# Storing the first blocks' column parts one step later, behind the reads of a pair's moves

## The chip, the core and the metric

The kernel runs on one core of a Trainium2 chip. The metric is the device time of one execution in microseconds, lower is better. The core has five engines that run side by side: TensorE (PE, matmuls), VectorE (DVE), ScalarE (ACT), GpSimd (POOL) and SyncE (SP), which here issues nearly all DMA transfers. Each engine takes its own instructions in program order, and waits on the others through semaphores.

## The reference

A block of a transformer: layer norm, then linear attention and a squared-ReLU MLP side by side, both added to the input. There are 2,048 tokens of 512 values, 32 heads of 16, and a hidden width of 1,376.

```python
xn = layernorm(x)
q, k, v = split_heads(xn @ wqkv)             # H = 32, Dh = 16
pq, pk = phi(q), phi(k)                      # phi(t) = where(t > 0, t + 1, exp(t)) + 1e-6
kv  = einsum("bhsd,bhse->bhde", pk, v)       # sums over all tokens
z   = einsum("bhsd->bhd", pk)
o   = einsum("bhqd,bhde->bhqe", pq, kv) / (einsum("bhqd,bhd->bhq", pq, z)[..., None] + 1e-6)
out = x + merge_heads(o) @ wo + (relu(xn @ w1 + b1) ** 2) @ w2 + b2
```

## The kernel before

The tokens are cut into 16 tiles of 128 rows, and four tiles make a block. Every matmul operand is held as a high and a low part (suffixes `h` and `l`), and a product is three matmul passes over these parts.

The order of work is written out by hand: nothing is rescheduled, and each engine runs its instructions in the order in which the program names them. The first third of the time is a loop over steps i = 2 to 15, one tile a step. It computes the keys of tile i and adds to the sum over all tokens that linear attention needs. A step's instructions for TensorE are:

- `project(i)`, 12 matmuls (line 370): the keys of tile i, from the tile's column parts `xs0` or `xs1`, into `pk`;
- for the first tiles, four transposes on TensorE (`pt`, line 309);
- `kx(i - 1)`, 12 matmuls (line 390): the tokens of the tile before times its keys.

The column parts of tile i are its normalised values turned by 128 x 128 and split into high (ScalarE, line 325) and low (VectorE, line 328). Block 0 (tiles 0 to 3) uses `xs1`, block 1 (tiles 4 to 7) `xs0`, block 2 again `xs1`, and so on. So `xs1` is overwritten from tile 8 on (in step 6) and `xs0` from tile 12 on (in step 10). `transposed(i)` does the turn. Tiles 0 to 4 are turned by TensorE. From tile 5 on the turn takes another way, through DRAM:

- the normalised tile, `xp`, is written to a DRAM buffer `via` (`regroup`, line 282). From tile 6 on, tiles go in pairs: (6, 7), (8, 9), ... In the text, via(7) or via(9) is the write of the pair that ends with that tile, issued in the step that normalises it;
- `regroup` also lists four reads `xg<-via`, each for 32 partitions. The text calls them the pair's moves. They are issued by `move()` at the head of the next step (line 290), and the first waits on SP until the write has landed;
- VectorE turns 32 x 32 blocks of the regrouped tile in SBUF (line 294), and then the high and low parts are made as before.

A tile i + 2 of this kind is transposed at the end of step i, so tile 6 at the end of step 4, and tile 8 at the end of step 6.

SP also issues, in this loop: the stores of the turned tiles 0 to 7 to `xTd` (line 337, each at the end of its `transposed`), the loads of `b1s` at the head of step 5 (ahead of `move()`), and the two stores `xsd` for each of blocks 0 and 1, 1 MB each, high and low parts. These keep the column parts of those blocks for the second half of the kernel, which reads them back (`xs0h<-xsd1h` and so on, issued from 223 us on). `fetch()` issues up to three loads of `wo` and `wqkv` pieces ahead; in steps 3 to 10 it has three outstanding and issues none.

After the loop, and until the end, the kernel computes queries, the hidden layer and the sums into the output, for two blocks at a time, twice. This part is not touched by the change.

Of the kernel before, what the change touches and what calls it, by code (L numbers as in the profile page):

```python
# [18 lines left out]
def kernel(  # L19
# [30 lines left out]
    nc = tc.nc  # L50
# [6 lines left out]
    TB = 4  # L57
# [20 lines left out]
    def bank(name, tag="ps"):  # L78
        return psum.tile([P, 512], F32, name=name, tag=tag)
# [14 lines left out]
    def four(name, tag, dt=F32, pool=None):  # L94
        return (pool or work).tile([P, TB, 512], dt, name=name, tag=tag)

    def pair(name):
        return keep.tile([P, 2, 512], F32R, name=name, tag=next_tag("pair"))

    def f32(ap):  # L100
        return ap.bitcast(F32)
# [15 lines left out]
    def split(h, l, src, eh, el):  # L117
        copy(eh, h, src)
        ENG[el].tensor_tensor(out=l, in0=src, in1=f32(h), op=OP.subtract)  # L119
# [27 lines left out]
    xsd = [[dram.tile([P, NJ, BT], F32, name=f"xsd{b}{u}") for u in "hl"] for b in range(NB // 2)]  # L147
# [25 lines left out]
    def units(f):  # L173


        if f < NF - 1:
            return [(0, f * P, P)]
        return [(0, f * P + Q, 2 * Q), (2 * Q, f * P, Q), (3 * Q, f * P, Q)]

    def raw_1(f):  # L180
        t = w512(f"r1_{f}", "raw", 6)
        tj = t.rearrange("p (j n) -> p j n", j=NJ)
        for a, o, n in units(f):
            nc.sync.dma_start(tj[:, :, a:a + n], w1[:, o:o + n].rearrange("(j p) n -> p j n", j=NJ))
        return t
# [47 lines left out]
    def statistics(*tiles):  # L233
        g = group(*tiles)
        measure(g)
        return g

    def roots(tiles, st, mv, y):

        n = len(tiles)  # L240
        nc.scalar.activation(y[:, 1, :n], mv[:, :n, 1], AF.Ln, bias=eps)
        nc.scalar.activation(y[:, 0, :n], y[:, 1, :n], AF.Exp, scale=-0.5)
# [44 lines left out]
    def move(n=8):  # L287
        for _ in range(n):
            if moves:
                nc.sync.dma_start(*moves.pop(0))  # L290
# [9 lines left out]
    def cols(i):  # L300

        return xsb[(i // TB + 1) % 2]
# [10 lines left out]
    def transposed(i, n=1):  # L313

        b, at = i // TB, slot(i)
        if i < NDVE:
            t = turned_pe(i, n)
        else:
            t = [xT[b][:, :, at] if i >= NPE else w512(f"t{i}", "p", 6).rearrange("p (j t) -> p j t", j=NJ)]
            turn(t[0], xg[i])  # L320
        m = NJ // n
        h, l = ([x[:, k * m:(k + 1) * m, at] for k in range(n)] for x in cols(i))

        def high(k=0):
            nc.scalar.activation(h[k], t[k], AF.Copy)

        def low(k=0):
            nc.vector.tensor_tensor(out=l[k], in0=t[k], in1=f32(h[k]), op=OP.subtract)

        def keep_t():  # L330
            o = t[0]
            if i < NDVE:
                o = w512(f"t{i}", "p", 6).rearrange("p (j t) -> p j t", j=NJ)
                for k in range(n):
                    copy("act", o[:, k * m:(k + 1) * m], t[k])
            if i < NPE:
                nc.sync.dma_start(xTd[b][:, :, at], o)

        return high, low, keep_t

    def run(*what):
        for f in what:
            f()
# [23 lines left out]
    def project(i, ps, w, steps, first=True, last=True):  # L367

        for n, (j, u, v) in enumerate(steps):
            nc.tensor.matmul(ps, lhsT=cols(i)[u][:, j, slot(i)], rhs=w[v][:, j, :], start=first and n == 0,  # L370
                             stop=last and n == len(steps) - 1)
# [8 lines left out]
    def phi_k(i, ps, mid=lambda: None, late=lambda: None):  # L380
        kp[i] = w512(f"k{i}", "p", 6)
        phi(ps, kp[i], mid, late)
# [159 lines left out]
    for i0 in range(0, NT, TB):  # L542
# [6 lines left out]
        if i0 < NPE:  # L549
            i = i0 + TB - n - 1  # L550
# [4 lines left out]
        for k in range(0, n, 2):  # L555
            i = i0 + TB - n + k
            u, v = (t.rearrange("p a (g c) -> p (a g c)", g=NJ) for t in (a[:, TB - n + k:][:, :2], o[:, k:k + 2]))
            groups[i + 1] = [t.rearrange("p (g n) -> p g n", g=NJ) for t in (u, v)]
            u, v = (t.rearrange("p (g i c) -> p g i c", g=NJ, i=2) for t in (u, v))
# [87 lines left out]
    def tokens_sum(n, tag):  # L647
        return keep.tile([P, 2, 2, 512], F32R, name=f"T{n}", tag=tag)
# [13 lines left out]
    def halves(t):  # L662

        return t[:, :2], t[:, 2:]
# [16 lines left out]
    def fetch():  # L681
        while todo and len(held) < 3:
            held.append(todo.pop(0)())
# [16 lines left out]
    def load_1(kind, n):  # L700
        load = raw_1 if kind == "w" else raw_q
        return [load(2 * n + k).rearrange("p (c n) -> p c n", c=2) for k in range(2)]
# [30 lines left out]
    def sums_of(f1, f2, o3, o4):  # L733


        o, sums = {}, []

        def sum_1(j):
            o[1] = difference(1, j, f2[:, j], f1[:, j])
            difference_high(1, j, o[1])  # L740

        def sum_2(j):
            o[2] = difference(2, j, f2[:, 2 + j], o[1])
            difference_high(2, j, o[2])

        for j in range(2):
            sums += [lambda j=j: sum_1(j), lambda j=j: sum_2(j),
                     lambda j=j: difference(4, j, f1[:, 2 + j], o[2], o4[:, j]),
                     lambda j=j: difference(3, j, f2[:, 2 + j], f2[:, j], o3[:, j]),
                     lambda j=j: difference_low(1, j, o[1]), lambda j=j: difference_low(2, j, o[2])]  # L750
        return sums

    def operands_first(n, w):

        o = {}

        def first():
            aop.update({k: keep.tile([P, 2, 2, 512], F32R, name=f"aop{n}_{k}", tag=f"xT{NB // 2 + k}") for k in range(2)})
            chunk_split(0, 0, w[0])

        def sums():
            o[0], o[1] = chunk_sums(0, w)

        return [first, sums, lambda: chunk_split(0, 1, o[0]), lambda: last_split(0, w[1][:, 1]),
                lambda: chunk_split(1, 0, o[1])]
# [7 lines left out]
    def more(i=None):  # L773

        if i is None or i > 12:
            do(extra, counts[0].pop(0))
# [6 lines left out]
    for i in range(2, NT):  # L783
        if i == 5:
            nc.sync.dma_start(b1s[:, :NF - 1], b1[:(NF - 1) * P].rearrange("(f p) -> p f", p=P))
            for a, o, n in units(NF - 1):
                nc.sync.dma_start(b1s[a:a + n, NF - 1:], b1[o:o + n, None])
        move()
        fetch()
        ps = pks[i] if i < 3 else bank(f"pk{i}")  # L790
        if i > 2:
            project(i, ps, wk, HL)
        high = low = keep_t = lambda: None
        if i < NDVE:
            high, low, keep_t = transposed(i + 1)

        soon_turned = transposed(i + 2) if 11 <= i and i + 2 < NT else ()

        def mid():
            high()  # L800
            more(i)

        def late():
            if soon:
                roots(*soon)
            low()
            more(i)

        if i == 12:
            rawz = raw_1(NF - 1)  # L810
            T.update({n: tokens_sum(n, f"B{n - 1}") for n in (1, 2)})
        if i == 12:
            w = load_1("q", 0)
        if i == 13:
            todo_1 = operands_first(0, w)
            extra.append(todo_1.pop(1))
        if i == 14:
            z = pair("w1z0")
            extra.append(lambda: split(z[:, 0], z[:, 1], rawz, "act", "dve"))
            o34 = halves(four("Tf", "r0"))  # L820
            extra.extend(sums_of(xT[NB - 1], xT[NB - 2], *o34))
            lows = [extra.pop() for k in range(2)]
            extra += [todo_1[0], lows[1], todo_1[1], lows[0], *todo_1[2:]]
        phi_k(i, ps, mid, late)
        more(i)
        run(*soon_turned)
        later = normalise(*soon) if soon else []
        parts(i)
        keep_t()
        if i == 2:  # L830
            tokens(2)
        if i + 1 < NT:
            tokens(i + 1)
        run(*later)
        if NDVE < i + 2 < 13:
            run(*transposed(i + 2))
        pieces([3, 1, 1, 2, 1][i - 11] if i > 10 else 0)
        if i == 2:
            ahead[3] = statistics(6, 7)
        if i + 2 in (4, 6, 8, 10):  # L840
            ahead[i + 2] = group(i + 6, i + 7)
        if i < 10:
            measure(ahead[(i + 2) // 2 * 2], i % 2)
        soon = ahead.get(i + 1, ())
        if i in (3, 6):

            b = i // 6
            for u in range(2):
                nc.sync.dma_start(xsd[b][u], f32(cols(b * TB)[u]))
        kx(i - 1)  # L850
        more(i)

# [52 lines left out]
    for n in range(2):  # L905
# [339 lines left out]
        for e, f in enumerate(waiting[:-2]):  # L1245
# [14 lines left out]
            if n == 0 and 1 <= e < 5:  # L1260
                k, u = divmod(e - 1, 2)
# [68 lines left out]
```

## Time and profile before

| | |
|---|---|
| time, median of 3 runs | 419.6 us (419.21 to 420.58) |
| time of the profiled execution | 419.62 us |
| its span, first to last instruction | 417.9 us |
| TensorE busy | 409.5 us, 98% |
| VectorE, ScalarE, GpSimd busy | 315.5, 269.9, 49.0 us |
| mean granted TensorE clock | 0.996 of full |
| DMA, mean over the span | 132 GB/s |

How to read what follows: the page's engine rows give busy time, share of the span and number of instructions. A row of the waits names the waiting instruction, what it waited for, the total in us, how often, and the longest. A row of a timeline gives start in us, duration in us, engine, line, operation, output and input, number of merged instructions, and in brackets the idle time before it with what ended it. Here `SPq` is SP's issue of a DMA; its duration is that of the issue, not of the transfer. A row of the chain gives start, duration and what. A row of the windows gives the stretch, its length, the busy time of PE, PE's weight loads, DVE, ACT and POOL with their instruction counts, and then the granted clock, the busy share of the DMA engines and GB/s. For one tile the durations are min/median/max, in ns for instructions and in us for the time from a DMA's issue to its landing.

### The profile page before, as it was taken

Reading aid. Unit: us, or ns where it says so; the run is one execution under the profiler, and the core shown is the slowest. Engines: PE = TensorE matmul, PEld = TensorE weight load, DVE = VectorE, ACT = ScalarE, POOL = GpSimd, SP = SyncE. Lnnn points to the kernel's source line nnn. Section 1 sums busy time; section 2 is a strip of 40 time slices with the busy share of each in tenths; the row PEclk is TensorE's granted clock in tenths of the full one; section 3 lists DMA queues with packets and bytes.
Section 4 is the critical chain, followed back from the end, with each engine's and each line's share of the span. In section 5 each row is a group of like instructions: output and inputs, shape, how many; then the busy total and the mean of one; then the engine's idle time right before and its main releaser. Section 6 shows DMA issues by size and latency. Waiting matters only on the chain.

```text
span 417.9 us, 5430 instructions
## 1 busy us (share of the span) xinstructions
PE 409.5 (98%) x1831; PEld 338.2 (81%) x1831; DVE 315.5 (75%) x585; ACT 269.9 (65%) x486; POOL 49.0 (12%) x70
## 2 busy tenths in 40 slices
PE   8998899999999999999999999999999999999996
PEld 7786788878888888888878888888888888878885
DVE  6893766699699898997539997467998685449843
ACT  5864776764778778889565732467678857737420
POOL 3241221221040000011000040100000200000210
PEclk9999899999999999999999999999999999999999
DMA  7869482460231222346076991511231781025602
GB/s 244 289 230 345 128 301 100 140 189 1 66 112 51 51 76 78 100 152 101 14 314 226 343 249 49 165 52 25 55 94 30 217 186 50 2 77 175 102 0 100
DMA packets 45645, 55.15 MB, mean 132 GB/s; under 512 B 7985, under 2 KB 29745, under 8 KB 44338
## 3 DMA queue, kind: packets, MB, share of 16 engines
q1 hardware_dynamic: 43314, 50.61, 37.5%
q0 software_dynamic: 2304, 4.20, 6.3%
q8 instruction: 14, 0.23, 0.2%
q14 instruction: 13, 0.11, 0.1%
HBM read 41.43 MB, written 13.37 MB: 131 GB/s over the span
## 4 chain that ended last, share of the span: by engine, by line
PE 93%; DMA 3%; DVE 1%; SPq 1%; ACT 1%; issue 0%; DVEq 0%
PE acc L130 36%; PE b L489 32%; PE pk L370 10%; PE kx L390 9%; PE acc L500 2%; DMA xg<-via 1%; PE pz L130 1%; PE pkv L881 1%; SPq L290 1%; PE pm L130 1%; DMA via<-xp 1%; PE pz0b L130 1%; PE b L130 1%; DMA x<-in_A_x_dram 1%; PE pt L309 0%
## 5 line engine op out<-in xcount | busy, mean ns | idle before, releaser
L130 PE MATMUL acc<-w2r,s 128*128 128x512 f32 x477 | 112.8, 390 | 0.0
L130 PEld LDWEIGHTS acc<-w2r,s 128*128 128x128 f32 x477 | 89.5, 188 | 19.2 <-issue 0.7
L489 PE MATMUL b<-T,aop 128*128 128x512 f32 x336 | 83.4, 390 | 0.0
L489 PEld LDWEIGHTS b<-T,aop 128*128 128x128 f32 x336 | 63.1, 188 | 13.1
L390 PE MATMUL kx<-pk,tok 128*128 128x512 f32 x192 | 46.6, 392 | 0.0
L390 PEld LDWEIGHTS kx<-pk,tok 128*128 128x128 f32 x192 | 36.0, 189 | 8.2 <-issue 0.4
L489 PE MATMUL b<-xs0h,aop 128*128 128x512 f32 x112 | 36.9, 391 | 0.0
L130 PE MATMUL acc<-mh,aTsr 128*128 128x512 f32 x112 | 35.7, 390 | 0.0
L1011 POOL DMA_DIRECT2D res<-in_B_b_dram x16 | 14.1, 1065 | 181.7 <-DVE dt L431 64.3
L119 POOL TENSOR_TENSOR tok<-xp,tok 128x512 fp32r<-128x512 f32 x16 | 21.4, 1342 | 61.9 <-ACT tok L111 61.9
L1019 DVE TENSOR_TENSOR res<-acc,res 128x512 f32<-128x512 f32 x16 | 11.0, 692 | 23.1 <-PE acc L130 18.4
L122 DVE TENSOR_TENSOR w2r<-r,w2r 128x512 fp32r<-128x512 f32 (+2 forms) x35 | 25.6, 734 | 0.1
L130 PEld LDWEIGHTS acc<-mh,aTsr 128*128 128x128 f32 x112 | 21.0, 188 | 4.4
L489 PEld LDWEIGHTS b<-xs0h,aop 128*128 128x128 f32 x112 | 21.0, 188 | 4.3
L111 ACT ACTIVATE aop<-S 128x512 fp32r<-128x512 f32 x28 | 17.5, 624 | 10.6 <-DVE S L710 10.6
L119 DVE TENSOR_TENSOR aop<-S,aop 128x512 fp32r<-128x512 f32 x28 | 19.5, 698 | 4.8 <-ACT aop L111 4.4
L119 DVE TENSOR_TENSOR s<-c,s 128x512 fp32r<-128x512 f32 x20 | 13.6, 690 | 11.5 <-ACT s L111 11.4
L130 PE MATMUL acc<-ml,aTsr 128*128 128x512 f32 x56 | 21.8, 390 | 0.0
L489 PE MATMUL b<-xs0l,aop 128*128 128x512 f32 x56 | 21.8, 390 | 0.0
L111 ACT ACTIVATE w2r<-r 128x512 fp32r<-128x512 f32 x32 | 19.6, 618 | 2.2 <-DMA out_dram<-res 2.0
L111 ACT ACTIVATE T<-Tf 128x512 fp32r<-128x512 f32 x16 | 9.5, 626 | 16.9 <-DVE Tf L653 16.7
L489 PE MATMUL b<-xs1h,aop 128*128 128x512 f32 x56 | 19.5, 390 | 0.0
(197 smaller groups left out, 771.8 us busy)
## 6 DMA issues: line engine op xcount, KB each, us to landing
r<-in_B_w_dram SPq DMA_DIRECT2D x49, 256.0 KB, 3.0
res<-in_A_x_dram SPq DMA_DIRECT2D x8, 512.0 KB, 4.7
res<-in_B_b_dram POOLq DMA_DIRECT2D x16, 256.0 KB, 5.4
out_dram<-res SPq DMA_DIRECT2D x15, 256.0 KB, 2.0
x<-in_A_x_dram SPq DMA_DIRECT2D x5, 512.0 KB, 5.2
via<-xp SPq DMA_DIRECT2D x5, 512.0 KB, 2.7
xg<-via SPq DMA_DIRECT2D x20, 128.0 KB, 3.5
xTd<-t SPq DMA_DIRECT2D x8, 256.0 KB, 3.0
```

Source lines behind the costliest of these rows:

```text
L111: nc.scalar.activation(o, i, AF.Copy, bias=bias)
L119: ENG[el].tensor_tensor(out=l, in0=src, in1=f32(h), op=OP.subtract)
L122: nc.vector.tensor_tensor(out=l, in0=src, in1=f32(h), op=OP.subtract)
L130: nc.tensor.matmul(ps, lhsT=a[u], rhs=b[v], start=first and n == 0, stop=last and n == 2)
L290: nc.sync.dma_start(*moves.pop(0))
L370: nc.tensor.matmul(ps, lhsT=cols(i)[u][:, j, slot(i)], rhs=w[v][:, j, :], start=first and n == 0, stop=last and n == len(steps) - 1)
L390: nc.tensor.matmul(kxp[c], lhsT=tok[i][:, u, c * P:(c + 1) * P], rhs=pk[i][:, v], start=i == 0 and (u, v) == first, stop=i == NT - 1 and ( ...
L489: nc.tensor.matmul(ps, lhsT=a[u][:, j * P:(j + 1) * P], rhs=b[v][:, j, :], start=first and j == 0 and n == 0, stop=last and j == 1 and n == 2,
L500: nc.tensor.matmul(ps, lhsT=s[u][:, k * P:(k + 1) * P], rhs=w2s[NF - 1][u][:, a:z], start=first and u == 0, stop=stop and u == 1)
L881: nc.tensor.matmul(ps[:, at], lhsT=wvs[:, c, at], rhs=kxs[c // 2][:, c % 2, at], start=c == 0 and j == 0, stop=c == NJ - 1 and j == NJ - 1 ...
L1011: nc.gpsimd.dma_start(r[:, i], b2[None, :].partition_broadcast(P), accum_op=OP.add)
L1019: nc.vector.tensor_tensor(out=r[:, a:z], in0=ps, in1=r[:, a:z], op=OP.add)
```

## The change

The two stores `xsd` of a block are taken from the end of step 3 (block 0) and step 6 (block 1), where they stand ahead of `kx(i - 1)`, and put at the head of steps 4 and 7, between `move()` and `fetch()`. The code between the old and the new place issues no DMA other than the moves. For SP this is an exchange: four moves and two stores change places, twice. The data, the sizes, the queue and all work of the other engines are as before.

```diff
@@ -786,6 +786,11 @@
         move()
+        if i in (4, 7):
+
+            b = i // 7
+            for u in range(2):
+                nc.sync.dma_start(xsd[b][u], f32(cols(b * TB)[u]))
         fetch()
...
@@ -842,11 +847,6 @@
         soon = ahead.get(i + 1, ())
-        if i in (3, 6):
-
-            b = i // 6
-            for u in range(2):
-                nc.sync.dma_start(xsd[b][u], f32(cols(b * TB)[u]))
         kx(i - 1)
```

## The prediction

> **What bounds the kernel now.** I read the page first, then the waits of TensorE, the chain of waits, and the timelines of the engines around the place that the chain points to.
>
> ```profile
> span 417.9 us, 5430 instructions
> PE 409.5 (98%) x1831; PEld 338.2 (81%) x1831; DVE 315.5 (75%) x585; ACT 269.9 (65%) x486; POOL 49.0 (12%) x70
> ...
> PE 93%; DMA 3%; DVE 1%; SPq 1%; ACT 1%; issue 0%; DVEq 0%
> ```
>
> TensorE is busy for 409.5 of 417.9 us and carries 93% of the chain, so a change of DMA order can only pay where TensorE stands still or runs slowly. Its waits over the whole run name one such place; all others are 0.8 us or less. The timeline of TensorE gives the place, the windows its clock.
>
> ```profile
> PE pk L370 <- ACT xs0h L325: 3.3, 1, 3.3
> PE warm L520 <- PEq L1316: 0.8, 1, 0.8
> ...
> 36.86 2.88 PE L390 MATMUL kx<-pk,tok 128*128 128x512 f32 x12
> 43.01 0.50 PE L370 MATMUL pk<-wkh,xs0h 128*128 128x512 f32 x1 [3.27 <-ACT xs0h L325]
> ...
> 44.00:47.40 3.40, 3.40 (x9) 2.61 (x9) 2.40 (x5) 1.44 (x4) 1.02 (x1) 0.51 0.53 91
> 47.40:50.00 2.60, 2.60 (x13) 2.15 (x12) 2.06 (x5) 2.07 (x5) 0.35 (x2) 0.98 0.75 227
> ```
>
> The 12 matmuls of kx(4) end at 36.86 + 2.88 = 39.74. The next instruction, the first of project(6), starts at 43.01, 3.27 us later, because the high part of tile 6 is missing. One microsecond after the gap the granted clock falls to 0.51 for 3.4 us, and then it is back at 0.98. The chain shows what tile 6 waits for (start, duration, what).
>
> ```profile
> 29.63 2.74 DMA via<-xp
> ...
> 32.39 0.74 SPq L290
> ...
> 35.77 5.69 DMA xg<-via
> ...
> 41.58 0.72 DVE t L294
> ...
> 42.33 0.64 ACT xs0h L325
> ...
> 43.01 4.61 PE pk L370 x12
> 47.62 2.73 PE kx L390 x12
> 50.34 2.72 PE pk L370 x12
> ```
>
> The pair (6, 7) is written to DRAM at 29.63, has landed at 32.37, and its four moves xg<-via are issued from 32.39. The last is issued at 35.77 and lands at 41.46. Then VectorE turns tile 6, ScalarE takes its high part, and TensorE goes on. After the gap project takes 4.61 us where the next one, at 50.34, takes 2.72. The whole price of the stall is 3.27 + (4.61 - 2.72) = 3.27 + 1.89 = 5.16 us. What stands ahead of the moves is seen in SP's timeline.
>
> ```profile
> 30.65 0.74 SPq L849 DMA_DIRECT2D xsd0h<-xs1h  x1
> 31.44 0.45 SPq L849 DMA_DIRECT2D xsd0l<-xs1l  x1
> 32.39 4.56 SPq L290 DMA_DIRECT2D xg<-via  x4
> 36.99 0.52 SPq L337 DMA_DIRECT2D xTd<-t  x1
> 37.62 0.65 SPq L282 DMA_DIRECT2D via<-xp  x1
> 42.32 0.53 SPq L337 DMA_DIRECT2D xTd<-t  x1
> 42.90 0.62 SPq L785 DMA_DIRECT2D b1s<-in_B_b_dram  x1
> 43.57 1.88 SPq L787 DMA_DIRECT2D b1s<-in_B_b_dram  x3
> 45.55 1.79 SPq L290 DMA_DIRECT2D xg<-via  x4
> ...
> 53.01 0.42 SPq L849 DMA_DIRECT2D xsd1h<-xs0h  x1
> 53.52 0.74 SPq L849 DMA_DIRECT2D xsd1l<-xs0l  x1
> 55.30 3.98 SPq L290 DMA_DIRECT2D xg<-via  x4
> 63.15 0.34 SPq L282 DMA_DIRECT2D via<-xp  x1
> ```
>
> Two stores of 1 MB each go out at 30.65 and 31.44, inside the time in which SP would only wait for the landing at 32.37; the moves stand behind them. The same four moves cost as follows without stores ahead (first pair of lines, the moves at 45.55) and with them (second pair, those at 32.39): issue durations, then issue to landing.
>
> ```profile
> L290 SPq DMA_DIRECT2D xg<-via x4: 367/430/432, 45.5 to 46.9; - x4
> ...
> DMA to landing us min/median/max: 2.4/2.6/2.7
> ...
> L290 SPq DMA_DIRECT2D xg<-via x4: 737/1210/1270, 32.4 to 35.8; - x4
> ...
> DMA to landing us min/median/max: 5.7/6.7/7.4
> ```
>
> From first issue to last landing that is 46.9 - 45.5 + 2.7 = 4.1 us in quiet, and 41.46 - 32.39 = 9.07 us behind the stores.
>
> **The change, part by part.** No instruction is added or removed. Four DMA issues move past eight, in two places.
>
> First place, step 4. The moves still can't start before 32.39, since via(7) lands at 32.37. With nothing ahead of them they take the quiet 4.1 us: landed at 36.5. Had they to share the DMA engines with the stores that now follow from about 34.2 (32.39 + 1.79), the far end is today's 41.46; I take the quiet value, since the stores come after them in the same queue.
>
> ```profile
> 34.76 0.69 DVE L378 SCALAR_TENSOR_TENSOR pk<-k,pk 128x512 fp32r<-128x512 f32 x1
> 41.58 0.71 DVE L294 STREAM_TRANSPOSE t<-xg 128x512 f32<-128x512 f32 x1 [6.12 <-DMA xg<-via]
> ...
> 45.87 0.69 DVE L378 SCALAR_TENSOR_TENSOR pk<-k,pk 128x512 fp32r<-128x512 f32 x1 [0.75 <-ACT pk L111]
> ...
> 35.16 1.51 ACT L259 ACTIVATE xp<-x,y 128x512 f32<-128x512 f32 x2
> ```
>
> VectorE is free from 35.45 and ScalarE from 36.67, so nothing else holds tile 6. Landing to TensorE took 43.01 - 41.46 = 1.55 us; 36.5 + 1.55 = 38.05 is 1.7 us before project(6) is due at 39.74. The gap goes, and with it the slow stretch behind it. What could be late next is kx(5), due at 39.74 + 2.72 = 42.46. Its last operand, the low part of pk(5), ended 45.87 + 0.69 - 42.33 = 4.23 us after the high part of tile 6 began; that would be 37.3 + 4.2 = 41.5, which is 0.9 us early. So the first place gives 5.16 us.
>
> The stores now stand behind the moves and ahead of the store xTd of tile 5 and of via(9), the pair (8, 9). Nobody waits for tile 5's store until the second half. But via(9) is the next pair's way to TensorE:
>
> ```profile
> DMA to landing us min/median/max: 5.7/5.7/5.7
> ...
> 32.40:37.60 5.20, 5.20 (x25) 4.31 (x24) 2.54 (x7) 3.81 (x8) 1.34 (x2) 1.00 1.08 398
> ```
>
> The first line is via(9) of before: it landed at 37.62 + 5.7 = 43.3, already behind stores and moves (ScalarE's xp lets it start no sooner than 36.67). The block of stores and moves ahead of it now begins with the moves at 32.39 and not with the stores at 30.65, so it starts 1.74 us later and I let via(9) land as much later, at 45.1. The near end is 43.3, if the engines catch up. The b1s loads, which held SP until 45.45, are now issued inside this wait, since the store of tile 6 ahead of them no longer waits for the late turn. The moves of pair (8, 9) then go out at 45.1 instead of 45.55 and land at 45.1 + 4.1 = 49.2. TensorE is 5.16 us earlier, however: project(8) is due at 39.74 + 4 x 2.72 = 50.62, and needs the landing by 50.62 - 1.55 = 49.07. That leaves 0.1 us of stall. The tile store xTd(6) and b1s may now still drain ahead of these moves: 256 KB at the 398 GB/s of the last column is 0.66 us, of which I take half. I put the new stall at 0.35 us. Its ends: nothing, if via(9) lands at 43.3; and 3 us more, if these moves land in 5.7 us (the best of the congested row) and not 2.7, which is 3.1 us.
>
> Second place, step 7: the stores at 53.01 and 53.52 go behind the moves at 55.30. They filled a wait of SP there too, and the moves behind them held VectorE, not TensorE, which has no wait in this stretch. Moves that land sooner give nothing. The stores go out some 4 us later, at 57.1 (55.30 + 1.79), ahead of the via issued at 63.15. Were that block to drain no faster than the one in step 4, in 9.07 us, the via would land 3 us later; I cost it at zero, because the pair behind stores in this same stretch cost TensorE nothing.
>
> The stores themselves read xs1, which step 6 overwrites with tile 8's parts. They were issued 1 us before the moves' wait ended; behind 1.79 us of moves they go out at 34.2 to 35.4 and precede via(9) in the queue, so tile 8, which needs via(9), comes after them. No wait is added there.
>
> Sum, against the profiled execution's 419.62 us (span 417.9, and 1.7 us around it; the median of the runs is 419.6): 419.62 - 5.16 + 0.35 = 414.8 us.
>
> **The rivals.** (a) *The gap moves one pair on, and is larger.* The moves of pair (8, 9) meet the stores that now come 3.5 us later: if they take the 9.07 us measured behind stores, they land at 45.1 + 9.1 = 54.2, project(8) stalls 54.2 - 49.1 = 5.1 us and the clock falls again for 1.89: 419.62 - 5.16 + 5.1 + 1.89 = 421.5 us. It decides from a landing at 49.07 + 3.27 = 52.3 on. For it: the margin computed above is nil. Against it: SP issues those moves only after via(9) has landed, and via(9) follows the stores in the queue, so the stores are gone by then. (b) *The same, in part*: a stall of 1 to 3 us at project(8), too short for the clock: 415.5 to 417.5. (c) *The stores take the engines anyhow*, and the moves land no sooner than 41.46 although issued ahead: 419.6. Against it: issue alone shrinks from 4.56 to 1.79 us, and what is issued first has the engines alone for 1.8 us. (d) *The slow clock stays*: the stretch of 0.51 is not due to the gap; then only 3.27 comes back: 414.8 + 1.89 = 416.7. The row speaks against it, with full clock on both sides and the fall right after the only gap of that size.
>
> The Trainium skill, page "TensorE: Matmul & The Clock Gate", section "What's actually happening", has the clock halve after at least one idle window of about 3.4 us. By that rule a gap of 3.27 us would be too short, and (d) would hold. The trace disagrees: the clock was 0.51 after just that gap.
>
> **How the numbers follow.** Forecast, with a new stall of 0 to 1 us: 0.72. (a) 0.09, (b) 0.10, (c) 0.06, (d) 0.03. A measurement here can tell about 0.3%, 1.3 us, from no change: faster means below 418.3. Forecast, (b) and (d) are faster, 0.85; (c) is the same, 0.06; (a) is slower, 0.09. The range starts at 414.0, which is no new stall (414.5) less the 0.4 us by which runs of before lie under their median, and reaches to 417.0, which takes in (d) and most of (b) and leaves out (a), (c) and the end of (b), under 0.2.
>
> **What would show it.** In the changed kernel's SP timeline the four moves at about 32.4 should take about 1.8 us with the stores behind them, and the turn of tile 6 should start at about 36.6. TensorE should have no wait at project(6) and no clock below 0.9 from 36 to 50, and kx(4) to kx(5) should be 5.44 us apart. The moves of pair (8, 9) should land at about 49, and a wait at project(8), if any, should be under 1 us. The forecast is wrong if tile 6 still lands after 38.2, if a wait of over 1 us stands at project(8), or if the half clock is seen without a gap ahead of it.

## The result, and the profile after

The changed kernel takes 414.12 us (median of 4 runs, 414.02 to 414.55) against 419.47 us before (4 runs, 419.21 to 420.58). The ratio is 0.987, with a 95% interval of 0.985 to 0.9889: 5.4 us faster. The forecast was 414.8 us in a range of 414.0 to 417.0. The profiled execution took 414.14 us, with a span of 412.4 us, which is 5.5 us less.

The page of the kernel after: span, engines, the granted clock in 40 slices, and the chain by engine.

```profile
span 412.4 us, 5429 instructions
...
PE 407.2 (99%) x1831; PEld 336.9 (82%) x1831; DVE 315.4 (76%) x585; ACT 269.8 (65%) x486; POOL 49.1 (12%) x70
...
PEclk9999999999999999999999999999999999999999
...
PE 97%; DVE 1%; DMA 1%; ACT 0%; issue 0%
```

DMA has fallen from 3% to 1% of the chain, and no slice shows a lower clock. Before, the fifth slice did:

```profile
PEclk9999899999999999999999999999999999999999
```

TensorE's waits of the kernel after, longest first:

```profile
PE warm L520 <- PEq L1316: 0.8, 1, 0.8
PE pt L309 <- DVE y L250: 0.7, 1, 0.7
PE pk L370 <- ACT xs1h L325: 0.3, 1, 0.3
```

The wait of 3.3 us on `xs0h` is gone, and nothing has taken its place. SP's timeline of the kernel after shows the exchange:

```profile
32.64 1.73 SPq L290 DMA_DIRECT2D xg<-via  x4
34.41 0.43 SPq L793 DMA_DIRECT2D xsd0h<-xs1h  x1
34.89 0.43 SPq L793 DMA_DIRECT2D xsd0l<-xs1l  x1
...
36.72 1.08 SPq L282 DMA_DIRECT2D via<-xp  x1
37.90 1.23 SPq L337 DMA_DIRECT2D xTd<-t  x1
39.18 1.44 SPq L785 DMA_DIRECT2D b1s<-in_B_b_dram  x1
40.68 3.33 SPq L787 DMA_DIRECT2D b1s<-in_B_b_dram  x3
44.11 1.79 SPq L290 DMA_DIRECT2D xg<-via  x4
```

From issue to landing, these four moves:

```profile
DMA to landing us min/median/max: 2.3/2.6/2.7
```

The moves take 1.73 us to issue instead of 4.56, and 2.7 us at most to land instead of 7.4. The transfers behind the stores pay for it: the issue of via(9) takes 1.08 us instead of 0.65, and that of the b1s loads 4.8 us instead of 2.5. VectorE's turns of tiles 6 and 8 show what that does:

```profile
36.76 0.71 DVE L294 STREAM_TRANSPOSE t<-xg 128x512 f32<-128x512 f32 x1 [1.28 <-DMA xg<-via]
...
48.49 0.71 DVE L294 STREAM_TRANSPOSE xT<-xg 128x512 f32<-128x512 f32 x1 [1.89 <-DMA xg<-via]
```

and so does the chain, from kx(4) on:

```profile
36.98 2.72 PE kx L390 x12
39.70 2.72 PE pk L370 x12
42.42 2.72 PE kx L390 x12
...
50.58 2.72 PE pk L370 x12
```

Tile 6 is turned at 36.76 instead of 41.58. Tile 8's moves now make VectorE wait 1.89 us, where it did not wait before. But project(8) still starts on time, at 50.58, and from kx(4) on TensorE runs through at 2.72 us for each group of 12, so kx(4) and kx(5) are 5.44 us apart, as forecast.

Where the 5.46 us between the two chains' last pieces (414.44 before, 408.98 after) come from can be read off: 5.20 us are gained by the start of project(8) (55.78 against 50.58). The rest is at kx(12), the 12 matmuls behind project(13); the chain has it so before:

```profile
85.72 2.98 PE kx L390 x12
```

and so after:

```profile
80.50 2.74 PE kx L390 x12
```

With the 0.02 us of issue ahead of the first, that is 0.26 us. (The expectations below call these matmuls kx(13), which is a miscount by one.)

### The profile page after: what moved, and what is told of

Same layout as the page of the kernel before. It is cut to its first block, busy times and chain, and to the rows that moved or that the text cites. A ratio compares the mean times of both kernels' runs of the same rounds, so it can differ in the third digit from the quotient of the medians.

```text
span 412.4 us, 5429 instructions
## 1 busy us (share of the span) xinstructions
PE 407.2 (99%) x1831; PEld 336.9 (82%) x1831; DVE 315.4 (76%) x585; ACT 269.8 (65%) x486; POOL 49.1 (12%) x70
## 4 chain that ended last, share of the span: by engine, by line
PE 97%; DVE 1%; DMA 1%; ACT 0%; issue 0%
PE acc L130 37%; PE b L489 32%; PE pk L370 11%; PE kx L390 11%; PE acc L500 2%; PE pz L130 1%; PE pkv L881 1%; PE pm L130 1%; PE pz0b L130 1%; PE b L130 1%; DMA x<-in_A_x_dram 1%; PE pt L309 1%; PE acc L507 0%; DVE st L230 0%; PE end L130 0%; DVE xp L269 0%
```

## The experiments

In each diff below, `...` stands for lines left out, and the comments are the document's.

**Which of the two places.** Each place was changed alone. The first alone, against the changed kernel:

```diff
-        if i in (4, 7):
+        if i == 4:
...
+        if i == 6:                 # block 1's two stores stay at the end of step 6
```

> Only block 0's stores go behind the moves of step 4; block 1's stay at the end of step 6. Theory: the whole gain comes from the first place, so 414.1 us, no wait of TensorE at project(6), and VectorE waits some 2 us for the moves of the pair (10, 11) as before the change. Rival (the second place pays for the 0.3 us that the gain exceeded 5.16 by, because a store ahead of moves in step 6 disturbs a later pair): 414.4 us, with kx(13) at 2.98 us instead of 2.72.

Measured: 414.38 us (414.21 to 414.84), ratio 0.9882 (0.9866 to 0.9899). The chain has project(6) and kx(12) so:

```profile
39.79 2.72 PE pk L370 x12
...
80.59 2.72 PE kx L390 x12
```

There is no wait at project(6), and kx(12) takes 2.72 us, where the rival gave 2.98. So the theory holds by the chain; the time alone could not tell 414.1 from the rival's 414.4. VectorE's wait for tile 10 was 0.94 us, where some 2 us were expected.

The second alone, against the changed kernel:

```diff
-        if i in (4, 7):
+        if i == 7:
...
+        if i == 3:                 # block 0's two stores stay at the end of step 3
```

> Block 0's stores stay at the end of step 3; only block 1's go behind the moves of step 7. Theory: no gain, 419.5 us, with the 3.3 us wait at project(6) and half clock after it. Rival (the second place is worth 0.3 us): 419.2 us, and kx(13) takes 2.72 us.

Measured: 420.67 us median (417.84 to 421.2, 10 runs), ratio 1.0022 (1.0005 to 1.0039), with the 3.3 us wait at project(6). The same two groups in the chain of the profiled run, which took 419.24 us:

```profile
42.85 4.60 PE pk L370 x12
...
85.59 2.72 PE kx L390 x12
```

So the stall stays and there is no gain, as expected. But kx(12) takes 2.72 us here too, which was the rival's sign. The 0.26 us at kx(12) are gone with either place changed alone, so these runs put them to neither, and 0.3 us can't be told in this spread of times. The spread was not expected, and it goes with the mean granted clock of the run: 417.84 us at 1.000, 419.24 at 0.994, 419.84 at 0.996, and 420.6 to 421.2 at 0.990 or 0.991. Why seven of the ten runs had 0.990 or 0.991 is open. This is taken up below.

**How much of the stores stands ahead.** Block 0's stores were left ahead of the moves by one, by one and a half, and by three (a third one to a spare buffer that nobody reads).

```diff
+        if i == 3:                 # one ahead (the other behind the moves of step 4)
+            nc.sync.dma_start(xsd[0][0], f32(cols(0)[0]))
...
+            nc.sync.dma_start(xsd[0][1][:, :2], f32(cols(0)[1])[:, :2])   # one and a half
...
+            nc.sync.dma_start(spare, f32(cols(0)[1]))                     # three: both and this one
```

> One of block 0's two stores (1 MB) stays ahead of the moves, the other goes behind them; block 1's stores as after the change. Theory (the moves wait for the bytes ahead of them): four moves take 4.1 us with nothing ahead and 9.1 us with 2 MB, so 6.6 us with 1 MB: landed at 39.0, 0.8 us later than the 38.2 that TensorE can bear, a gap of 0.8 us without a fall of the clock: 414.9 us. Rival (any store ahead costs the whole, since the moves then share the engines with one): gap 3.3 us, 419.5 us. Second rival, the slow clock has another cause: half clock near 44 us without a gap of 3 us ahead of it, 416.8 us.

> One and a half of block 0's stores (1.5 MB) stay ahead of the moves, the last half goes behind; block 1's stores as after. Theory: 7.8 us to landing, a gap of 2.1 us at project(6). If the clock falls only after a gap of some 3 us, 416.2 us with full clock throughout; if a gap of 2 us is enough to halve it for 3.4 us, 418.1 us. Rival (any store ahead costs the whole): 419.5 us.

> All of block 0's stores stay ahead of the moves, and a third store of 1 MB, to a DRAM buffer that nobody reads, is added behind them and ahead of the moves; block 1's stores as after. Theory: 11.6 us to landing, a gap of 5.8 us at project(6). If the half clock lasts one stretch of 3.4 us whatever the gap, its price stays at 1.9 us and the time is 419.5 + 2.5 = 422.0 us; if the clock stays low for longer after a longer gap, two stretches cost 3.8 us and the time is 423.9 us. Rival (the stores' bytes are not what delays the moves, but the first store's presence): 419.5 us.

Measured: 415.04 us (414.64 to 415.15), ratio 0.9895 (0.9879 to 0.9911), with one store; 416.71 us (415.89 to 418.62, 9 runs), ratio 0.9943 (0.9923 to 0.9962), with one and a half; 422.23 us (421.82 to 422.47), ratio 1.0052 (1.0035 to 1.0069), with three. The first matmul of project(6) in TensorE's timeline, and the whole of project(6) in the chain, with one store ahead:

```profile
40.21 0.50 PE L370 MATMUL pk<-wkh,xs0h 128*128 128x512 f32 x1 [0.52 <-ACT xs0h L325]
```

```profile
40.21 3.02 PE pk L370 x12
```

with one and a half:

```profile
41.98 0.50 PE L370 MATMUL pk<-wkh,xs0h 128*128 128x512 f32 x1 [1.78 <-ACT xs0h L325]
```

```profile
41.98 3.02 PE pk L370 x12
```

and with three (its line numbers are one higher, for the line that makes the spare buffer):

```profile
45.33 0.80 PE L371 MATMUL pk<-wkh,xs0h 128*128 128x512 f32 x1 [5.68 <-ACT xs0h L326]
```

```profile
45.33 5.36 PE pk L371 x12
```

The gap grows with the bytes ahead: 0, 0.52, 1.78, 3.27 and 5.68 us for 0, 1, 1.5, 2 and 3 MB, where 0, 0.8, 2.1, 3.3 and 5.8 were expected. That is about 2.6 us for each MB beyond the first. Each gap is that of the one profiled run; with one and a half stores the runs at full clock lie between 415.89 and 417.6 us, so there it differs from run to run. "Any store ahead costs the whole" is refuted. A gap that leaves the clock alone still costs 0.3 us more than its length, because project(6) takes 3.02 us instead of 2.72.

With three stores the clock was low for longer, as the windows show (the granted clock is the third number from the end):

```profile
40.00:43.40 3.40, 0.00 (x0) 0.00 (x0) 0.00 (x0) 0.00 (x0) 0.00 (x0) 1.00 1.00 248
43.40:50.60 7.20, 5.27 (x13) 4.16 (x14) 4.52 (x8) 3.53 (x6) 1.36 (x2) 0.53 0.64 180
50.60:54.00 3.40, 3.40 (x17) 2.78 (x16) 2.83 (x9) 2.87 (x7) 0.02 (x1) 1.00 0.36 104
```

A mean of 0.53 over 7.2 us is some 6.8 us at half clock (7.2 x 0.47 / 0.5), two stretches of 3.4. Up to 1.9 us of it fall into the gap, which ends at 45.33. So project(6) lost only 5.36 - 2.72 = 2.64 us, between the 1.9 and 3.8 us that the expectation held against each other, and the time came out near the 422.0 us forecast for one stretch although there were two.

**The prediction's rival (a) made real.** Block 0's stores go behind via(9), and so ahead of the next pair's moves.

```diff
-        if i in (4, 7):
+        if i == 7:                 # block 1 as after; block 0 at the end of step 4:
...
+        if i == 4:
+            for u in range(2):
+                nc.sync.dma_start(xsd[0][u], f32(cols(0)[u]))
         kx(i - 1)
```

> Block 0's stores go to the end of step 4, behind via(9) and ahead of the moves of the next pair (8, 9); block 1's stores as after. This is the prediction's rival (a) made real: stores ahead of the moves of a pair, one pair on. Theory: via(9) now has nothing ahead of it and lands in under 3 us, by 39.6; the moves of (8, 9) go out only after the loads of b1s, near 43, and the stores ahead of them are done by about 45, so they land near 48, under the 49.1 that project(8) needs: 414.1 us, at most 0.5 us more. Rival (a): these moves take 9.1 us from there, land at 52 or later, project(8) stalls for 3 us and the clock halves: 419 us.

Measured: 417.44 us (415.75 to 417.8), ratio 0.9933 (0.9909 to 0.9957). My expectation was wrong: the gap did move one pair on, though with a smaller size than rival (a) gives. SP's timeline in this kernel:

```profile
38.25 0.64 SPq L850 DMA_DIRECT2D xsd0h<-xs1h  x1
...
39.44 1.12 SPq L785 DMA_DIRECT2D b1s<-in_B_b_dram  x1
40.59 4.14 SPq L787 DMA_DIRECT2D b1s<-in_B_b_dram  x3
44.78 1.84 SPq L290 DMA_DIRECT2D xg<-via  x4
```

the turn of tile 8 on VectorE:

```profile
50.71 0.71 DVE L294 STREAM_TRANSPOSE xT<-xg 128x512 f32<-128x512 f32 x1 [3.95 <-DMA xg<-via]
```

and the first matmul of project(8):

```profile
52.14 0.50 PE L370 MATMUL pk<-wkh,xs1h 128*128 128x512 f32 x1 [1.46 <-ACT xs1h L325]
```

The moves of (8, 9) go out at 44.78 because the b1s loads hold SP until then: issued behind the stores, these four loads take 5.3 us of SP's time instead of 2.5. But that is only 0.7 us later than in the changed kernel (44.11), and tile 8 is turned 2.2 us later (50.71 against 48.49). The rest is in the time from issue to landing of these moves, here and then in the changed kernel:

```profile
DMA to landing us min/median/max: 2.5/2.9/4.3
```

```profile
DMA to landing us min/median/max: 2.4/2.7/2.8
```

TensorE waits 1.46 us at project(8), and 1.0 us more at kx(7). To tell the b1s loads from the stores' bytes, the loads were moved to step 9, here and in the changed kernel.

```diff
-        if i == 5:                 # the four b1s loads, ahead of move()
+        move()
+        if i == 9:                 # the same four loads, behind move()
```

> As the kernel with block 0's stores at the end of step 4, with the four b1s loads moved from the head of step 5 to step 9, behind its moves. That kernel took 417.4 us because the moves of (8, 9) went out only at 44.8 and landed at 50.6. Theory (SP was held by the b1s loads, 5.3 us of issue behind the stores): the moves now go out from 39.6 on, when via(9) lands, and are in by about 46 to 48, no wait at project(8): 414.2 us. Rival (the stores' own bytes ahead of these moves are the cause, as in step 4 before the change): landed 9.1 us after via(9), near 49 or later, project(8) still waits: 415 to 417.5 us.

> The changed kernel, with the four b1s loads moved from the head of step 5 to step 9, behind its moves. Theory: TensorE has no wait left that hangs on them, so the time stays at 414.1 us within 0.3; the moves of (8, 9) go out when via(9) lands and VectorE's wait of 1.9 us for them becomes shorter. Rival (the b1s loads still cost TensorE something, through a late tile 8): 413.8 us or less.

Measured: 414.42 us (413.99 to 414.85), ratio 0.9877 (0.9858 to 0.9896), with the stores at the end of step 4, and 414.23 us (414.21 to 415.05), ratio 0.9879 (0.9856 to 0.9901), for the changed kernel. In the first, the moves of (8, 9) in SP's timeline:

```profile
39.51 4.62 SPq L290 DMA_DIRECT2D xg<-via  x4
```

and tile 8's turn in VectorE's:

```profile
48.69 0.71 DVE L294 STREAM_TRANSPOSE xT<-xg 128x512 f32<-128x512 f32 x1 [2.18 <-DMA xg<-via]
```

Tile 8 comes 2 us sooner, and the wait at project(8) is gone: the b1s loads ahead of the moves made the difference. Whether they did it by the time for which they held SP or also by their own transfers isn't separated. The moves themselves are as slow behind the stores as the rival had it: from 39.51 to about 48.6 is 9.1 us, the same as before the change. Issued that early, they are still in time. In the changed kernel the loads are worth nothing, as expected; neither version beats it. Without the loads its moves of (8, 9) go out when via(9) has landed:

```profile
44.31 1.74 SPq L290 DMA_DIRECT2D xg<-via  x4
```

That is no earlier than with them (44.11), in a run whose earlier moves went out 0.5 us later (33.12 against 32.64). So in the changed kernel the loads held these moves for only some 0.3 us beyond the landing of via(9).

**The clock by itself.** The kernel before, with 12 more matmuls for TensorE in the gap, whose result is overwritten.

```diff
+        if i == 6:
+            for n in range(12):
+                nc.tensor.matmul(ps, lhsT=wk[0][:, n % NJ, :P], rhs=wk[0][:, n % NJ, :], start=True, stop=True)
         if i > 2:
             project(i, ps, wk, HL)
```

> The kernel before, with 12 more matmuls whose result is overwritten (2.7 us of work for TensorE) ahead of project(6), where it otherwise stands idle for 3.3 us. The stores and moves stay as before. Theory: tile 6 comes no sooner, so the gap's own 3.3 us stays, but TensorE is idle for only 0.6 us of it and its clock doesn't fall: project(6) takes 2.7 to 3.0 us instead of 4.6, clock 1.00 in every run, 417.6 to 418.0 us. Rival (the slow stretch has another cause than the idle time): half clock near 44 us all the same, 419.5 us or more.

Measured: 419.22 us (418.74 to 419.66, 10 runs), ratio 0.9984 (0.9969 to 1.0). The clock is as expected, with a mean of 0.998 to 1.000 in every run; the size of the gain is not. In the profiled run 0.54 us of the gap are left idle. The windows:

```profile
44.00:47.40 3.40, 3.40 (x16) 2.63 (x15) 2.39 (x5) 1.43 (x4) 1.03 (x1) 1.00 0.55 84
```

VectorE's turn of tile 10:

```profile
63.86 0.71 DVE L294 STREAM_TRANSPOSE xT<-xg 128x512 f32<-128x512 f32 x1 [2.34 <-DMA xg<-via]
```

and project(10) in the chain:

```profile
65.29 3.06 PE pk L370 x12
```

The clock stays at 1.00 between 44 and 47.4. But via(11) goes out at 52.61 as before the change, since VectorE and ScalarE are no earlier. So tile 10, whose moves stand behind block 1's stores, is now late for TensorE: project(10) starts with a wait of 0.3 us and takes 3.06 us, and part of the gain is lost. Adding the second place of the change tests that.

```diff
+        if i == 6:                 # the filled gap, as above
...
+        if i == 7:                 # block 1's stores behind the moves of step 7
```

> The kernel with the filled gap (12 matmuls whose result is overwritten, ahead of project(6)), and block 1's stores behind the moves of step 7 as in the changed kernel; block 0's stores stay ahead of the moves of step 4. With the filled gap alone TensorE won 1.9 us at project(6), and gave some 0.6 us back at project(10), whose tile waits for moves behind block 1's stores. Theory (the second place matters as soon as TensorE is early enough): project(10) starts without a wait and takes 2.72 us, 418.6 us against 419.2. Rival (the second place never matters; the 0.6 us have another cause): 419.2 us, with project(10) as late as in the kernel with the filled gap.

Measured: 417.96 us (417.61 to 420.31, 10 runs), ratio 0.9964 (0.9944 to 0.9984). Eight runs had a mean clock of 0.999 or 1.000 and took 417.61 to 418.29 us; the other two had 0.996 and took 420.15 and 420.31.

The same row of the chain in this kernel:

```profile
65.22 2.72 PE pk L370 x12
```

project(10) no longer waits. The two profiled runs, both near full clock, are 0.8 us apart (417.91 and 418.74), where 0.6 was expected; the medians are 1.3 us apart, but the two kernels ran on different chips, and the intervals of their ratios overlap. kx(12) is back at 2.72 us here, where it took 3.00 with the filled gap alone. So the second place of the change matters when TensorE is earlier than VectorE and ScalarE are. With the first place changed, all engines are 5 us earlier together, and the runs show no use of it.

The two runs at 0.996 were not expected: with only 0.60 us of the gap left idle in the profiled run, the clock still fell in two of ten. No trace of these two is kept, so where it fell, and why, is open.

## Why the prediction was right, and where it was off

**The stall and its removal: right.** The four moves took 1.73 us to issue and 4.1 us from first issue to the turn, tile 6 was turned at 36.76 (36.6 forecast), and project(6) started at 39.70. The first place alone gives the whole gain, and the gap follows the bytes ahead of the moves.

**The new stall of 0.35 us: not there.** The step that failed is via(9). I let it land 1.74 us later than before, at 45.1; it landed at 36.72 + 7.1 = 43.8, near the end that I had put at 43.3. Its time to landing in the kernel after:

```profile
DMA to landing us min/median/max: 7.1/7.1/7.1
```

The b1s loads, which the prediction had hidden inside the wait for via(9), took 4.8 us to issue instead of 2.5 and ended at 44.01, 0.2 us after via(9) had landed. So both held the moves of (8, 9) until about the same time, 1 us before the forecast. The moves landed by 48.4 instead of 49.2, some 0.6 us before project(8) would have waited. The margin was as thin as that: with the stores at the end of step 4, tile 8 came 2.2 us later, and project(8) waited.

**The 0.26 us at kx(12)** were not in the sum. In the kernel before, VectorE turns tile 14 at 83.61, 2.1 us before kx(12) starts, and only then makes the last operand of kx(12); where tile 14 is turned 2.4 us ahead or more, as in the changed kernel, they are not there. They come and go between kernels. Why that turn was late is open. These 0.26 us and the missing stall are most of the difference between 414.8 and 414.12.

**The slow clock: right in the sum, wrong as a rule.** For the profiled execution 1.89 us was the difference. Not all of it was the clock's: the 12 matmuls behind a short gap take 3.02 us at full clock, so 0.3 us of it go with a gap at full clock too, and some 1.6 with the half clock. Nor is it a fixed price. Of 51 runs of the kernel before that stand beside the experiments, five had a mean clock of 1.000 and took 418.4 to 418.9 us; one had 0.999 and took 419.2; 29 had 0.994 to 0.996, with a median of 419.5; and 16 had 0.990 to 0.992, with a median of 420.6. So its time moves by some 2 us with the clock. That the stall at project(6) is behind all of this is likely, not shown: only the profiled run tells where the clock fell. The changed kernel has no such gap, and its runs lie within 0.5 us at clocks of 0.999 to 1.000. The filled gap shows the other half: keeping the clock up and changing nothing else was worth 0.4 us at the median, since the next late tile took over.

Rival (d) is refuted for the profiled stretch: with the idle time filled, or with the gap gone, the slow stretch near 44 us does not come. The two runs at 0.996 with the gap filled and the second place changed stay unexplained. My reading of the Trainium skill there ("TensorE: Matmul & The Clock Gate", section "What's actually happening") was too strict. The Trainium skill also says there that the window is free-running, which fits a fall that comes in some runs of a kernel and not in others. A window that must be idle for all of 3.4 us doesn't fit: with one and a half stores ahead, a gap of 1.78 us in the profiled run, the mean clock was 0.995 or 0.996 in 3 of 9 runs. Their times, 417.87 to 418.62 us, less the 1.6 us for a half clock give 416.3 to 417.0, within those of the runs at full clock, so I estimate that their gaps were no longer.

**Rivals (b) and (c)** did not come true: there is no wait at project(8), and tile 6 is turned at 36.76.

**Rival (a)** did not come true in the changed kernel. The kernel with the stores at the end of step 4 shows that its place was well chosen. Its price of 9.1 us to landing came back where the moves were issued straight behind the stores; where they went out at 44.78 they took about 5.9 us, and the stall was 1.46 us and not 5.1.

**The second place: zero, as forecast**, with the first one changed, to the 0.3 us or so that these runs can tell. Without the first, and with TensorE made earlier, it is worth about 1 us.

## What to carry to other kernels

A large store that nobody waits for isn't free just because the engine that issues it would only have waited. In these runs, what was issued behind it on SP landed later by some 2.6 us for each MB beyond the first, and the issue of small transfers behind it slowed down as well. No run issued the stores from another engine, so whether that would spare the transfers behind them is open. Look for the first transfer behind such a store that the bounding engine waits for, and put the store behind it; then follow the next such transfer, and all that holds the queue ahead of it, to its own deadline. When a stall goes, ask whether the other engines get earlier with the bounding one, or whether the next wait is already due.

## What the runs showed of the hardware

First, a gap in TensorE's work can halve its clock, and does so in some executions of a kernel and not in others. After the gap of 3.27 us the clock was at half for 3.4 us in the profiled run, and the mean clock was below 0.997 in 45 of 51 runs of that kernel. With a gap of 1.78 us in the profiled run it was so in 3 of 9. After a gap of 5.68 us the clock was at half for some 6.8 us. The kernels with gaps of 0.52 us and of 1.46 us in their profiled runs had 0.998 to 1.000 in four runs each, but with 0.60 us left idle two of ten runs had 0.996. These runs give no threshold.

Second, the issue of a DMA is itself slow behind queued stores: four b1s loads of 5 KB and less took 4.8 to 5.3 us of SP's time there, against 2.5 us in the kernel before, where they went out some 11 us behind the stores.
